# Gated attention feeding eight experts on one core: x written by engines instead of small transfers, outer products 128 wide, the plan made anew, the last plain products spread over the first groups

## The chip, the cores and the metric

The program runs on one core of a Trainium2 chip. The metric is the device time of one execution in microseconds (us). A median over several executions is compared; a profile shows one execution. The engines are TensorE (PE, with its weight loads listed as PEld), VectorE (DVE), ScalarE (ACT), GpSimd (POOL), and SyncE (SP), which here only issues DMA transfers.

## The reference

Gated linear attention over 4 batches, 8 heads, 768 tokens and 48 channels, and behind it 8 experts whose outputs are mixed with weights that come from eight rounds of row and column scaling:

```
f = sigmoid(f_logit)
for t in range(S):                       # per batch and head, state is 48 x 48
    state = f[t][:, None] * state + k[t][:, None] * v[t][None, :]
    y[t] = q[t] @ state
x = y as [3072 tokens, 384]
P = exp(x @ w_gate - max); 8 times: P /= rowsum; P /= colsum; P *= N / E
out = sum over e of P[:, e] * (relu(x @ w1[e]) @ w2[e])      # w1 384 x 1024, w2 1024 x 384
```

## The kernel before

All large products are made of float16 pairs, a high and a low part, as three matmuls (high by high, high by low, low by high), summed in float32 in PSUM.

**The stages.** The order of the instructions of every engine is fixed in the program. A first stage follows the string `PLAN`, a list of words that each emit one step of one stream. There are 24 tiles of 128 tokens (six per batch), and each tile `i` has the streams `L` (loads), `K` (keys), `d` (decays), `Q`, `V`, `A` (scores), `S` (states), `c` (carried state), `Y` (output y and x), `g` (gate logits), all in `attend`. `F` emits plain products of experts on tokens that are ready, namely those of expert 0 and of half of expert 1; they are the filler of the plan. `E` and `D` emit their evictions. `C0` to `C3` (`convert`) turn the x of a batch into sums of blocks; `B` is the scaling chain of the expert weights; `k0` and `k1` prepare the first expert weights of the second stage. After the word `X`, behind the last tile, the buffers of the attention are given back.

The second stage runs 52 periods (`period`), one per entry of `ORDER`. Each has 15 slots with six matmuls each, which are products by a scheme that forms 15 products of sums of blocks; the second half of an expert (`paired`) follows 21 slots behind. `EVENTS` says which engine step comes behind which slot, and further jobs are hung on slots by `at_all` with the lists `W1AT`, `W2AT0`, `CONVAT` and so on. The last 24 plain products are held back from the plan and emitted in the first nine slots by the counts in `HELD`.

**A token tile on its way.** `outer(c)` forms the products of keys and values in the PSUM tile `kvps`: per half of a tile 12 matmuls with a stationary operand that is R = 112 columns of `ktb`, the turned keys, wide, and 48 moving columns. The state, with the carried one, goes by DVE and ACT into `sh` and `sl`, and `outputs` collects 48 matmuls into the PSUM tile `yps`. It has one buffer, like `kvps`. Then x is written as `xh` and `xl` (float16, 128 rows: 96 rows of the first three blocks of `yps`, and three pieces of 32 rows out of its fourth block, which have to land on rows 96 to 127). In the first six tiles ACT writes the four parts of `xh` and DVE the four parts of `xl`. From tile `X3_FROM` = 6 on the 96 rows of the fourth block go into a staging tile `x3` first (one ACT, one DVE instruction), and six transfers issued by SP move its pieces of 32 rows to their places. `gates` then multiplies x by the gate weights, into spare columns of the same `kvps` buffer; the next tile's `outer` needs that buffer.

The matmuls of all these are issued through one helper (L374), the ACT steps of a tile through L648, its DVE and POOL steps through L651 and L654, and the transfers of x at L827.

Of the kernel before, what the change touches and what calls it, by code (L numbers as in the profile page):

```python
# [60 lines left out]
L0 L1 a0 a1 a2 B a3 a4 a5 a6 a7 G z K0 K0 W24 K0 K0 Z Z V0 Z V0 K0 Z K0 V0 V0 K0 V0 K0 V0 K0 K1 d0 T0 U0 V1 W3 K0 z Q0 V1 T0 T0 W3 d0 T0 Q0 U0 U0 S0  # L61
L2 Q0 W4 S0 U0 Q0 S0 c0 S0 S0 V1 A0 S0 c0 V1 V1 W9 K1 A0 V1 a0 K1 A0 K1 a0 K1 Y0 d1 Y0 a1 A0 b0 Q1 K1 Y0 d1 Y0 a2 Y0 Q1 Y0 S1 a1 Y0 Y0 Y0 Y0 F2 Q1 F2
Y0 F3 b1 F1 K1 F3 Q1 F1 Y0 Y0 K1 Y0 F1 K1 F1 a3 F3 L3 T1 U1 F4 T1 F1 K1 F6 U1 F5 a2 F3 a4 T1 A1 a3 E T1 D a5 a4 U1 a6 F8 a5 F3 b2 F1 U1 F7 a7 F5 a6 F2
b3 F7 K2 F5 a7 F1 E F3 V2 F1 D F1 G F3 V2 V2 F3 V2 A1 V2 F1 g0 K2 F2 g0 V2 F1 S1 A1 K2 c1 K2 F1 K3 A1 Y1 Y1 V3 F2 S1 F1 K2 S1 F2 E d2 Y1 c1 b0 K2 S1
V3 S1 S1 Q2 S1 Y1 Y1 K2 Q2 Y1 K2 K2 Y1 L4 U2 K2 Y1 T2 Y1 Y1 F2 Q2 Y1 F5 Y1 F1 T2 T2 Y1 Q2 F2 Y1 F2 U2 F2 b0 g1 T2 F2 U2 F2 d2 F1 A2 U2 S2 V3 F2 g1 F3
A2 V3 F1 S2 c2 V3 S2 F3 A2 F1 S2 F5 c2 F4 S2 F3 A2 Y2 Y2 E F5 V3 F3 D F5 S2 F1 Y2 F1 S2 F1 K3 F3 Y2 S2 Y2 b1 F4 K3 F3 Y2 F1 K3 F4 Y2 F3 E b1 F1 d3 F2
Y2 F1 Y2 F1 Y2 K3 F1 D F3 d3 Y2 b2 F1 S3 F2 Y2 F1 Y2 F1 b3 F1 Y2 F1 K3 F3 K4 g2 b2 F2 K3 F8 g2 F1 b3 E F7 K3 K3 F10 V4 F8 K4 F3 V4 F6 K3 E F9 V4 F3 D
F5 V4 F8 V4 F3 K3 F6 E F8 V4 F3 D F5 Q3 F13 K4 K4 F4 E F5 D K4 d4 F3 Q3 F1 d4 F3 K4 F1 Q3 L5 F1 S3 F1 K4 Q3 S3 F1 K4 F1 S3 K4 F1 S3 F1 Q4 F1 A3 K4 F2
c3 F1 S3 F2 A3 F5 E F6 Q4 F2 A3 F1 S4 F2 K4 F6 S3 S3 F2 L6 F6 Q4 F2 Y3 A3 F2 K5 Y3 S3 F2 E F1 Q4 F1 Y3 V5 F1 D F1 K5 Y3 F1 A4 V5 V5 V5 K5 Y3 V5 F2 Y3
V5 F1 A4 F1 Y3 F7 E F7 Y3 F2 Y3 F3 Y3 Y3 F3 A4 F6 Y3 F3 Q5 Y3 F4 Y3 F2 A4 F1 E F3 Q5 K5 g3 K5 Y4 d5 F1 D F1 d5 Q5 Y4 F2 g3 K6 K5 Y4 F2 K6 Q5 S4 F1 K5  # L70
S4 S4 F1 S4 F1 E F1 c4 F1 S4 K6 F1 S5 F2 S4 F2 K5 F2 S4 F1 K5 F1 V6 Y4 F4 E S4 Y4 F2 Q6 F10 K6 F2 K6 K5 F9 V6 F1 V6 F7 V6 F2 Y4 F2 E F1 d6 F2 K5 F2 L7
F4 Y4 F1 A5 D Y4 Y4 Y4 Y4 F2 V6 F6 Y4 F1 V6 F3 Y4 F3 Y4 F2 d6 F2 A5 F8 E F2 g4 Q6 F4 A5 F5 D F3 Q6 F8 g4 F1 A5 F2 Y5 K7 F4 Y5 K6 S5 K7 F1 Y5 Q6 K6 S5
F2 S5 F1 E S5 F2 K7 F1 S5 F3 S5 F2 K6 K6 F1 D F3 V7 Y5 S5 F1 K7 K7 F1 Y5 K6 F1 Q7 F1 S5 F6 d7 F1 K6 F1 L8 E F1 V7 A6 V7 V7 K7 Y5 F1 V7 F1 A6 F1 Y5 F3
Q7 Y5 F1 Y5 F1 Y5 F1 A6 Y5 F7 E F1 Y5 F4 Y5 F2 V7 F1 C0 F1 Y5 F3 A6 F3 K7 F7 g5 K7 Y6 g5 F4 Y6 Q7 K7 F3 S6 E Q7 Y6 S6 d7 K8 F2 K7 D F8 V8 F2 S6 F5 c6
F3 S6 F2 C0 V8 F2 K7 F1 S6 F1 L9 F3 V8 F2 A7 V8 Y6 K8 F5 S7 F1 Y6 F1 E F5 S6 F4 V8 F3 C0 F5 V8 F1 D F11 A7 F7 E S6 F2 C0 F1 A7 F1 D F2 K9 F1 Y6 C0 A7
F2 Y6 F1 Y6 F1 Y6 F1 K8 K8 F1 K9 F6 Y6 F1 d8 Q8 F2 C0 C0 F2 E F1 Y7 C0 K8 F1 Q8 g6 Y7 d8 C0 F1 g6 F1 K8 Q8 Y7 F1 C0 F1 S7 F1 K9 K9 S7 K8 F3 K8 F1 K8
F7 E F6 V9 F1 S7 F5 S7 F2 K9 F9 K8 F5 c7 F5 E V9 F8 S7 F6 S8 F2 K8 S7 F2 L10 F5 D F1 V9 F6 d9 F2 V9 F2 S7 Y7 F1 E F3 Y7 S7 F2 V9 F4 D F3 V9 F6 Y7 K9
d9 F5 Y7 F2 Y7 F1 Q8 F6 K9 F2 Y7 F1 C0 C0 F1 E F1 A8 Q9 C0 D F1 K9 F1 K9 F1 Y7 F1 K10 F2 A8 F1 K10 F2 K9 g7 Q9 F1 A8 F2 g7 F1 K10 Q9 F2 C0 F1 K9 K10
L11 Y8 S8 Y8 S8 A8 F1 K10 d10 F2 C0 F1 S8 V10 F1 S8 F2 E Y8 c8 F1 S8 F1 V10 F1 S9 F1 S8 F1 S8 F2 V10 F6 E Y8 S8 F2 V10 F2 Y8 K10 F2 V10 F7 V10 Y8 Q9
F5 Y8 F2 C0 C0 Y8 F7 K10 F3 A9 C0 Y8 K10 F2 Y8 K10 F4 E F4 A9 F4 Q10 F7 D F1 K10 F2 A9 F8 Q10 F1 d10 F2 K11 F6 g8 A9 C0 Y9 K10 E L12 F4 Y9 g8 Q10 C0 D  # L80
# [24 lines left out]
K22 F1 Y19 F1 d22 E F2 Y19 Y19 F1 D F2 K22 F1 Y19 F2 d22 F1 E K22 F2 Q22 F2 D Y20 K22 F1 Q22 F1 Y20 K22 F1 K22 g19 Y20 E g19 F2 A21 F1 D F1 S20 K22
Q22 F1 A21 S20 K23 F1 S20 F2 S20 V22 F1 K22 F1 c20 F1 E F1 V22 S21 F1 S20 F2 D F1 S20 F1 S20 F2 V22 F1 S20 F1 E F1 Y20 Q22 V22 F2 Y20 V22 D F2 V22 Y20
# [239 lines left out]
def fast(ctx, tc, qkf, vbd, wg, w1, w2, out, flag):  # L346
# [140 lines left out]
    def put(e, u, t, ps):  # L487
# [6 lines left out]
        if t == TT - 1:  # L494
            over.add((e, u))
# [472 lines left out]
    def convert(b, raw_left):  # L968
# [15 lines left out]
        if not planned[0]:  # L984
            yield
# [531 lines left out]
```

## Time and profile before

| | us |
|---|---|
| median of 3 runs | 1539.29 (1539.0 to 1542.9) |
| the profiled execution | 1545.27 |
| its span, first to last instruction | 1543.5 |
| TensorE busy in it | 1477.4 |

The first 381 us hold the attention (the last logits of a tile are reduced at 381.0), from there to 467 us run the rest of the plain products beside the scaling chain, and at 467 us the periods begin. The busy times by stretch show how far each engine is filled; the table of waits says what ended TensorE's idle time; the timeline shows single steps. A matmul's listed duration includes its way through the array, so that neighbours overlap: the distance between their starts is what one costs TensorE.

### The profile page before, as it was taken

What the parts mean: (1) busy time and instruction counts of PE and PEld (TensorE: products, weight loads), DVE (VectorE), ACT (ScalarE), POOL (GpSimd) and SP (SyncE); (2) the same over time, 40 slices, a digit from 0 to 9 for tenths busy, and PEclk for the clock granted to TensorE, in tenths of its full rate; (3) what the DMA queues carried; (4) which work ended last, traced back from release to release, by engine and by line L of the source; (5) the groups of instructions that cost most, each with busy time, mean ns of one, the idle gap of its engine ahead of it and who ended that gap; (6) DMA issues with size and microseconds to landing.
All of it is one profiled execution on the core that took longest, in us unless ns stands there. A gap on an engine that the chain in (4) does not pass through costs nothing.

```text
span 1543.5 us, 41018 instructions
## 1 busy us (share of the span) xinstructions
PE 1477.4 (96%) x16128; PEld 1302.3 (84%) x16128; DVE 1256.5 (81%) x2549; ACT 1157.3 (75%) x2600; POOL 1062.2 (69%) x1259
## 2 busy tenths in 40 slices
PE   8898889988999999999999999999999999999997
PEld 5776766665567899999999999999999999999997
DVE  6887777664946998888999998888888888888876
ACT  8886887763337778888888888887777778777774
POOL 3234343312725569999999999999888888888763
PEclk9999999999999999999999999999999999999999
DMA  8354435521111012222111111111000000000012
GB/s 255 89 131 117 120 96 120 130 77 32 37 42 47 12 28 58 59 59 58 58 53 58 53 49 52 51 45 37 22 13 21 22 12 22 22 22 22 1 48 81
DMA packets 87419, 89.87 MB, mean 58 GB/s; under 512 B 54992, under 2 KB 74576, under 8 KB 87216
## 3 DMA queue, kind: packets, MB, share of 16 engines
q1 hardware_dynamic: 86784, 86.57, 20.2%
q8 instruction: 128, 2.10, 0.6%
q14 instruction: 75, 0.61, 0.1%
q10 hardware_dynamic: 432, 0.59, 0.1%
HBM read 62.46 MB, written 14.16 MB: 50 GB/s over the span
## 4 chain that ended last, share of the span: by engine, by line
PE 75%; DVE 5%; ACT 3%; DMA 3%; SPq 2%; issue 1%; ACTq 0%; DVEq 0%
PE kyps L374 29%; PE kb_A L374 9%; PE kb_B L374 8%; PE kb_D L374 6%; PE kxps L374 5%; PE kb_C L374 4%; PE hps L374 4%; PE yps L374 4%; PE kb_E L374 2%; PE kb_F L374 2%; PE kvps L374 2%; DMA xl<-x 2%; SPq L827 2%; DMA xh<-x 1%; ACT vh L648 0%
## 5 line engine op out<-in xcount | busy, mean ns | idle before, releaser
L374 PEld LDWEIGHTS <-k1h 128*128 128x128 f16 x3120 | 293.7, 98 | 27.4 <-issue 6.1
L374 PE MATMUL kyps<-k2h,kgh 128*128 128x192 f16 x1248 | 307.3, 246 | 1.5 <-ACT kyps L1219 1.5
L374 PE MATMUL kyps<-k2l,kgh 128*128 128x192 f16 x1248 | 307.4, 246 | 0.0
L374 PE MATMUL kyps<-k2h,kgl 128*128 128x192 f16 x1248 | 307.4, 246 | 0.0
L374 PEld LDWEIGHTS <-kgh 128*128 128x128 f16 x2496 | 230.0, 98 | 8.8 <-issue 1.8
L1392 POOL TENSOR_TENSOR kgl<-kf,kgh 128x512 f16<-128x512 f32 x153 | 205.7, 1345 | 2.5 <-ACT kgh L1389 2.5
L1222 DVE SCALAR_TENSOR_TENSOR yy<-kyps,pes,part 128x192 f32<-128x192 f32 x282 | 116.9, 415 | 101.2 <-PE kyps L374 91.1
L1392 POOL TENSOR_TENSOR kgl<-kr,kgh 128x512 f16<-128x512 f32 x153 | 182.2, 1191 | 11.5 <-PE kyps L374 9.9
L1261 POOL TENSOR_TENSOR acc<-acc,yy 128x384 f32<-128x384 f32 x141 | 141.1, 1001 | 67.7 <-DVE yy L1222 67.7
L374 PEld LDWEIGHTS <-k1l 128*128 128x128 f16 x1560 | 152.8, 98 | 17.8
L374 PEld LDWEIGHTS <-kh 128*128 128x128 f16 x1248 | 117.3, 98 | 8.9 <-issue 2.1
L374 PEld LDWEIGHTS <-kgl 128*128 128x128 f16 x1248 | 122.2, 98 | 0.1
L651 POOL TENSOR_TENSOR kb<-q,kb 48x512 f16<-48x512 f32 x42 | 51.8, 1234 | 86.4 <-ACT kb L648 85.1
L1343 ACT ACTIVATE cp<-kb_A 128x512 f32<-128x512 f32 x156 | 93.5, 599 | 20.0 <-DVE kb_A L1345 18.3
L1369 POOL TENSOR_TENSOR kr<-kr 128x256 f32<-128x256 f32 x104 | 78.0, 750 | 44.1 <-ACT kr L1358 41.7
L1219 ACT ACTIVATE kyps<-kyps 128x192 f32<-128x192 f32 x156 | 50.2, 322 | 73.0 <-PE kyps L374 70.9
L1389 ACT ACTIVATE kgh<-kf 128x512 f16<-128x512 f32 x156 | 98.7, 633 | 0.4 <-DVE kf L1366 0.4
L1389 ACT ACTIVATE kgh<-kr 128x512 f16<-128x512 f32 x156 | 98.1, 629 | 0.0
L374 PEld LDWEIGHTS <-w1h 128*128 128x128 f16 x1008 | 75.6, 101 | 25.0 <-issue 5.5
L374 PE MATMUL yps<-w2l,hh 128*128 128x384 f16 x288 | 95.9, 333 | 0.0
L374 PE MATMUL yps<-w2h,hl 128*128 128x384 f16 x288 | 95.9, 333 | 0.1
L374 PE MATMUL yps<-w2h,hh 128*128 128x384 f16 x288 | 95.6, 332 | 0.0
(287 smaller groups left out, 5531.2 us busy)
## 6 DMA issues: line engine op xcount, KB each, us to landing
q<-in_qkf_dram SPq DMA_DIRECT2D x23, 672.0 KB, 5.9
k1r<-in_w_dram SPq DMA_DIRECT2D x26, 384.0 KB, 3.0
k2r<-in_w_dram SPq DMA_DIRECT2D x26, 384.0 KB, 3.0
ys<-yr SPq DMA_DIRECT2D x48, 192.0 KB, 2.0
yb<-ys SPq DMA_DIRECT2D x48, 192.0 KB, 2.4
vr<-in_vbd_dram SPq DMA_DIRECT2D x24, 192.0 KB, 3.7
out_dram<-acc SPq DMA_DIRECT2D x21, 192.0 KB, 1.9
w1r<-in_w_dram SPq DMA_DIRECT2D x6, 384.0 KB, 8.5
```

The lines of the kernel that those rows point to most:

```text
L374: ins = (nc.tensor.transpose if transpose else nc.tensor.matmul)(**kw)
L651: pin(eng.tensor_tensor(out=out, in0=in0, in1=in1, op=op))
L827: nc.sync.dma_start(out=x[96:128, n, tok], in_=x3[32 * n:32 * n + 32, q, :])
L1219: pin(nc.scalar.activation(out=out, in_=in_, func=AF.Copy, **kw))
L1222: pin(nc.vector.scalar_tensor_tensor(out=y, in0=ps, scalar=p, in1=z, op0=ALU.mult, op1=ALU.add))
L1261: pin(nc.gpsimd.tensor_tensor(out=y, in0=y, in1=z.rearrange("p s d -> p (s d)"), op=ALU.add))
L1343: pin(nc.scalar.activation(out=fresh(ev[2]), in_=bk, func=AF.Copy))
L1369: pin((nc.gpsimd if ev[2] == 'P' else nc.vector).tensor_tensor(out=r[:, 0], in0=r[:, 1], in1=r[:, 0], op=ALU.subtract))
L1389: pin(nc.scalar.activation(out=hs['g', t][0][i], in_=hs['f' if i else 'r', t], func=AF.Copy))
L1392: pin((nc.vector if tag == str(PERIODS - 1) else nc.gpsimd).tensor_tensor(out=hs['g', t][1][i], in0=hs['f' if i else 'r', t], in1=hs['g', ...
```

## The change

In `outputs`, all 24 tiles write x the way the first six do: four ACT and four DVE instructions, no staging tile, no transfers. A step of the plan is one of these, so that the `Y` stream of tiles 6 to 23 has 14 steps in place of 10. `outer` takes a stationary operand 128 columns wide from tile 3 on (the first three tiles, turned by TensorE, stay at 112); the 16 further columns belong to the next block and their results are not read.

The plan is new over its whole length, with the same streams. Plain products ahead of the last tile's gate logits: 1855 before, 1875 after; in the whole plan 2352 before, 2340 after. Two new streams `k2` and `k3` prepare the first w2 weights in the plan (nine steps each); before they hung on the slots of the first period (`W2AT0`, `W2AT1`). Those weights get buffers of their own (`k2p`). The last conversion steps of batch 3 move from the second period to the first (`CONVAT`). A plain expert's tokens count as free when its first product is done, no longer when its second is. The 36 last plain products, in place of 24, are held and spread over the first 19 slots; the buffers that open behind them are split in two pools (`lq`). A check that tokens are ready is now made per block.

```diff
-HELD = (0, 1, 6, 2, 6, 3, 2, 4, 0)
-X3_FROM = 6
+HELD = (0, 0, 0, 0, 1, 1, 2, 2, 2, 3, 3, 3, 3, 3, 3, 3, 3, 2, 2)
-W2AT0 = (1, 1, 1, 2, 3, 4, 4, 4, 6)
-W2AT1 = (2, 8, 9, 11, 11, 12, 12, 12, 15)
-CONVAT = (0, 1, 6, 10, 12, 14, 15, 22, 24, 24, 26, 33, 35)
+CONVAT = (0, 1, 2, 3, 4, 5, 6, 7, 8, 9, 10, 11, 12, 13, 14)
...
         def outer(c):
-            kv = o["kv"][:, c]
+            kv, wide_ = o["kv"][:, c], R if by_pe else 128
...
-                    mm(out=kv[0:R, p, :], lhsT=ktb[i % 2][:, w:w + R], rhs=x[:, c * NP + p, :], start=(m == 0), stop=(m == 2))
+                    mm(out=kv[0:wide_, p, :], lhsT=ktb[i % 2][:, w:w + wide_], rhs=x[:, c * NP + p, :], start=(m == 0), stop=(m == 2))
...
-            parts = PCS
-            if i >= X3_FROM:
-                parts = PCS[:1]
-                x3 = new("x3", [96, 2, TS], F16, bufs=1)
-                act(x3[:, 0, :], yps[0:96, 3], scale=YS * XS)
-                yield
-            for n, (si, so) in enumerate(parts):
+            for n, (si, so) in enumerate(PCS):
                 act(xh[so + (tok,)], yps[si], scale=YS * XS)
...
-            if i >= X3_FROM:
-                three(x3[:, 1, :], yps[0:96, 3], YS * XS, x3[:, 0, :], ALU.mult, ALU.subtract)
-                for q, x in enumerate((xh, xl)):
-                    for n in range(3):
-                        nc.sync.dma_start(out=x[96:128, n, tok], in_=x3[32 * n:32 * n + 32, q, :])
-                ready.add((u, s % TT, 0))
-                yield
-            for n, (si, so) in enumerate(parts):
+            for n, (si, so) in enumerate(PCS):
                 three(xl[so + (tok,)], yps[si], YS * XS, xh[so + (tok,)], ALU.mult, ALU.subtract)
...
+    streams.update((f"k{2 + n}", prepare_w2(ORDER[0][0], 2 * ORDER[0][1] + n)) for n in range(2))
...
-        if n == 0:
-            at_all(0, W2AT0, prepare_w2(e, 2 * m))
-            at_all(0, W2AT1, prepare_w2(e, 2 * m + 1))
...
-    at_all(1, CONVAT, converts[3])
+    at_all(0, CONVAT, converts[3])
```

## Rows read from the trace of the kernel before

**Rows 1.** The page of the profile: the span, the busy time of each engine over it, and the clock granted to TensorE in 40 equal slices (tenths of full speed).
```profile
span 1543.5 us, 41018 instructions
...
PE 1477.4 (96%) x16128; PEld 1302.3 (84%) x16128; DVE 1256.5 (81%) x2549; ACT 1157.3 (75%) x2600; POOL 1062.2 (69%) x1259
...
PEclk9999999999999999999999999999999999999999
```

**Rows 2.** The busy time of each engine in six stretches of the span that follow one another. Columns: stretch and its length in us, busy us of PE, of the weight loads (PEld), of DVE, ACT and POOL, each with its number of instructions; then the granted clock of TensorE as a share, the busy share of the DMA engines and GB/s.
```profile
0.00:61.00 61.00, 48.57 (x597) 35.47 (x598) 44.26 (x81) 51.19 (x105) 19.11 (x36) 0.92 0.59 180
61.00:121.00 60.00, 56.31 (x912) 47.22 (x910) 50.76 (x79) 51.80 (x111) 23.19 (x22) 1.00 0.55 137
121.00:381.00 260.00, 227.57 (x2844) 166.72 (x2842) 170.42 (x304) 180.30 (x387) 82.21 (x98) 0.93 0.40 98
381.00:467.00 86.00, 83.52 (x520) 50.67 (x519) 58.64 (x121) 30.31 (x64) 43.14 (x61) 1.00 0.11 39
467.00:540.00 73.00, 67.36 (x637) 58.71 (x635) 60.84 (x118) 55.09 (x121) 42.02 (x55) 0.98 0.10 31
540.00:1543.50 1003.50, 994.02 (x10629) 943.47 (x10627) 871.52 (x1848) 788.62 (x1816) 852.58 (x990) 1.00 0.13 39
```

**Rows 3.** What TensorE's matmuls waited for in the stretch from 121 to 381 us. Columns: us in total, number of waits, the longest. `kvps` with `xl` or `xh` is a matmul of the gate logits; `yps` is the output of a token tile.
```profile
PE kvps L374 <- DMA xl<-x: 20.4, 43, 1.9
PE kvps L374 <- DMA xh<-x: 7.8, 9, 1.9
PE yps L374 <- DVE xl L654: 2.1, 4, 1.4
```

**Rows 4.** The timeline of SyncE's DMA issues around 170 us: start, duration in us, what, how many.
```profile
168.01 1.79 SPq L827 DMA_DIRECT2D xh<-x  x3
169.91 1.80 SPq L827 DMA_DIRECT2D xl<-x  x3
171.80 2.75 SPq L491 DMA_DIRECT2D ys<-yr  x2
```

**Rows 5.** The timeline of TensorE around 338 us: start, duration, matmul, and in brackets the idle time ahead of it with its releaser.
```profile
337.26 0.18 PE L374 MATMUL kvps<-wgs,xl 128*128 128x16 f16 x1 [0.46 <-DMA xl<-x]
...
338.59 0.18 PE L374 MATMUL kvps<-wgs,xl 128*128 128x16 f16 x1 [0.47 <-DMA xl<-x]
```

**Rows 6.** The busy times in slices of 3.4 us (columns as in Rows 2, the granted clock third from the end). Between 121 and 381 us 18 slices, in eight stretches, show a clock under 1.00; the first two, two in the middle and the last of these are given.
```profile
125.80:129.20 3.40, 2.38 (x28) 1.82 (x28) 1.91 (x3) 1.16 (x2) 0.55 (x2) 0.75 0.16 58
129.20:132.60 3.40, 3.40 (x30) 2.79 (x30) 1.07 (x3) 0.30 (x2) 2.01 (x2) 0.50 0.00 0
...
336.60:340.00 3.40, 1.96 (x24) 1.34 (x25) 1.72 (x4) 0.91 (x3) 0.59 (x1) 0.87 0.21 68
340.00:343.40 3.40, 3.40 (x32) 2.83 (x31) 0.47 (x2) 1.47 (x4) 0.00 (x0) 0.63 0.16 58
...
370.60:374.00 3.40, 3.40 (x19) 1.89 (x18) 1.82 (x4) 1.53 (x3) 0.00 (x0) 0.61 0.00 0
```

**Rows 7.** The costliest groups of weight loads from 0 to 640 us, shapes kept apart. `kt` is the turned keys of the outer products (112 columns), `kb` the keys of the scores (128 columns). Columns: busy us, mean ns of one, idle before.
```profile
L374 PEld LDWEIGHTS <-kt 128*112 128x112 f16 x576 | 41.5, 150 | 4.6 <-issue 2.1
...
L374 PEld LDWEIGHTS <-kb 112*128 112x128 f16 x624 | 24.0, 101 | 4.3 <-issue 2.5
```

**Rows 8.** The timeline of TensorE around 161 us. The first two rows bound one half of a tile's outer products (12 matmuls, then other work), the last two the scores of a tile (24 matmuls, then other work).
```profile
160.41 0.26 PE L374 MATMUL kvps<-vhc,kt 128*112 128x48 f16 x2
...
161.03 0.27 PE L374 MATMUL hps<-xl,w1h 128*128 128x128 f16 x2
...
162.12 0.22 PE L374 MATMUL aps<-qh,kb 112*128 112x64 f16 x2
...
162.82 0.84 PE L374 MATMUL hps<-xh,w1l 128*128 128x128 f16 x12
```

**Rows 9.** The timeline of ACT at token tile 3, whose x is written by engines already.
```profile
78.91 0.49 ACT L648 ACTIVATE xh<-yps 96x384 f16<-96x384 f32 x1
...
79.80 0.85 ACT L648 ACTIVATE xh<-yps 32x128 f16<-32x128 f32 x3
```

**Rows 10.** The timeline of DVE at the same tile: the low parts of x, four instructions in one row.
```profile
80.68 1.49 DVE L654 SCALAR_TENSOR_TENSOR xl<-yps,xh 96x384 f16<-96x384 f32 x4 [1.82 <-ACT xh L648]
```

**Rows 11.** The timeline of ACT at a later tile, whose last 96 rows go by transfers: the staging tile `x3` (printed as `x`), then `xh`.
```profile
167.72 0.26 ACT L648 ACTIVATE x<-yps 96x128 f16<-96x128 f32 x1
167.88 0.48 ACT L648 ACTIVATE xh<-yps 96x384 f16<-96x384 f32 x1
```

**Rows 12.** The timeline of DVE at the same later tile.
```profile
168.40 0.29 DVE L654 SCALAR_TENSOR_TENSOR x<-yps,x 96x128 f16<-96x128 f32 x1 [0.58 <-ACT xh L648]
...
169.20 0.55 DVE L654 SCALAR_TENSOR_TENSOR xl<-yps,xh 96x384 f16<-96x384 f32 x1
```

**Rows 13.** What TensorE's matmuls waited for from 61 to 121 us, where x is written by engines for nearly all of it (columns as in Rows 3).
```profile
PE yps L374 <- ACT sh L648: 1.4, 1, 1.4
PE kvps L374 <- DVE xl L654: 1.0, 2, 0.7
```

**Rows 14.** What TensorE's matmuls waited for from 467 to 540 us (columns as in Rows 3).
```profile
PE kb_A L374 <- ACT cp L1343: 2.4, 4, 1.4
PE kb_D L374 <- DVE kf L1366: 1.1, 2, 0.6
PE kb_D L374 <- DVE kb_F L1348: 0.9, 2, 0.7
```

More of the change, by code (lines that the diff above doesn't have):

```diff
@@ L65 @@
[L65 to L68, printed above, removed]
@@ L477, in evicted, with need @@
             yield
-    def need(u, parts, low):
-        if not all((u, t, low) in ready for t in parts):
+    def need(u, parts, low, k):
+        if not all((u, t, low, k) in ready for t in parts):
             raise RuntimeError("an expert is ahead of its tokens")
@@ L493, in put @@
         evict("E", op)
-        if t == TT - 1:
-            over.add((e, u))
     def moe_up(e, u, h, to=FT):
@@ L505, in moe_up @@
             for a, x in ((wh, xh), (wl, xh), (wh, xl)):
-                need(u, range(TT), int(x is xl))
                 for k in range(KT):
+                    need(u, range(TT), int(x is xl), k)
                     mm(out=ps, lhsT=a[:, k, fs], rhs=x[:, k, :], start=(n == 0), stop=(n == 8))
@@ L517, in moe_up @@
             hl.append(tl)
+            if f == FEATS[e] - 1:
+                over.add((e, u))
             yield 1
@@ L538, in tile_up @@
         w1s = ws[e][0]
-        need(u, (t,), 0)
         xh, xl = xof(u)
@@ L560, in tile_up @@
             h.append([v.rearrange("p (f t) -> p f t", t=128) for v in (th, tl)])
+            if t == TT - 1 and g == FEATS[e] // 4 - 1:
+                over.add((e, u))
             yield 1 / 3
@@ L811, in outputs @@
                 yield
-            parts = PCS
-            if i >= X3_FROM:
-                parts = PCS[:1]
-                x3 = new("x3", [96, 2, TS], F16, bufs=1)
-                act(x3[:, 0, :], yps[0:96, 3], scale=YS * XS)
-                yield
-            for n, (si, so) in enumerate(parts):
-                act(xh[so + (tok,)], yps[si], scale=YS * XS)
-                if n == len(PCS) - 1:
-                    ready.add((u, s % TT, 0))
-                yield
-            if i >= X3_FROM:
-                three(x3[:, 1, :], yps[0:96, 3], YS * XS, x3[:, 0, :], ALU.mult, ALU.subtract)
-                for q, x in enumerate((xh, xl)):
-                    for n in range(3):
-                        nc.sync.dma_start(out=x[96:128, n, tok], in_=x3[32 * n:32 * n + 32, q, :])
-                ready.add((u, s % TT, 0))
-                yield
-            for n, (si, so) in enumerate(parts):
+            for n, (si, so) in enumerate(PCS):
+                act(xh[so + (tok,)], yps[si], scale=YS * XS)
+                ready.add((u, s % TT, 0, n - 1))
+                yield
+            for n, (si, so) in enumerate(PCS):
                 three(xl[so + (tok,)], yps[si], YS * XS, xh[so + (tok,)], ALU.mult, ALU.subtract)
-                if n == len(parts) - 1:
-                    ready.add((u, s % TT, 1))
+                ready.add((u, s % TT, 1, n - 1))
                 yield
@@ L982, in block @@
             return sums[n // 9][:, n % 9, :].rearrange("p (u t) -> p u t", u=2)
-        if not planned[0]:
-            yield
         for i, (r, p, op, q) in enumerate(XSUMS):
             pin((nc.vector if b in SUMS_BY_DVE else nc.gpsimd).tensor_tensor(out=block(r), in0=block(p), in1=block(q), op=ALU.add if op == '+' else ALU.subtract))
-            if planned[0]:
-                yield
+            yield
             if i in (1, 5, 9):
@@ L992, in convert @@
                 pin(nc.vector.tensor_reduce(out=xmx[:, b, k:k + 1], in_=x32[:, k].rearrange("p u t -> p (u t)"), axis=AX.X, op=ALU.max, apply_absolute_value=True))
-                if planned[0]:
-                    yield
-            if i % 2 and not planned[0]:
                 yield
-        if not planned[0]:
-            yield
         xb = [xqs[b // 2].tile([128, 6, 256], F16, name=f"xb{n}{b}") for n in "hl"]
@@ L1002, in convert @@
                 pin(nc.scalar.activation(out=dst[:, 4 + n, :].rearrange("p (u t) -> p u t", u=2), in_=src[:, q // 3, :, 128 * (q % 3):128 * (q % 3) + 128], func=AF.Copy, scale=sign))
-                if planned[0]:
-                    yield
-            if not planned[0]:
                 yield
-        if not planned[0]:
-            yield
         while raw_left() > 0:
@@ L1018, in convert @@
                 pin(nc.scalar.activation(out=dst[0][:, lo:hi, :], in_=sums[n][:, lo:hi, :], func=AF.Copy))
-                if planned[0] and i:
+                if i:
                     yield
@@ L1083, in prepare_w2 @@
         yield
-        wh, wl = (lp.tile([128, 7, DH], F16, name=f"k2{n}_{e}_{j}", tag=f"k2{n}", bufs=4) for n in "hl")
+        place = len(turns) % 4
+        turns.append(place)
+        wh, wl = ((k2p if place < 2 else lp).tile([128, 7, DH], F16, name=f"k2{n}_{e}_{j}", tag=f"k2{n}{place}", bufs=1) for n in "hl")
         (b11, b12), (b21, b22) = ((raw[:, f, 0:DH], raw[:, f, DH:DM]) for f in range(2))
@@ L1158, in fast @@
             kw = ctx.enter_context(tc.tile_pool(name="kw", bufs=4, reuse_waits="tile"))
+            k2p = ctx.enter_context(tc.tile_pool(name="k2p", bufs=1, reuse_waits="tile"))
         elif word[0] == "F":
@@ L1178, in fast @@
     late.append(lp)
-    lq = []
+    lq = [ctx.enter_context(tc.tile_pool(name="lq", bufs=1, reuse_waits="tile"))]
     acc = {}
@@ L1192, in paired @@
         x0, y0, x1 = q[:, 0:DH], p[:, 0:DH], p[:, DH:DM]
-        p2 = lq[0].tile([128, DH], F32, name=f"part_{n}_{t}", tag="part", bufs=2)
+        p2 = lq[1].tile([128, DH], F32, name=f"part_{n}_{t}", tag="part", bufs=2)
         by_pool = t in BY_POOL and n < len(ORDER) - 1 and not new
@@ L1387, in event @@
                 else:
-                    hs['g', t] = [[lq[0].tile([128, 2, 2, 128], F16, name=f"kg{q}{i}_{tag}_{t}", tag=f"kg{q}{t}{i}", bufs=1) for i in range(2)] for q in "hl"]
+                    hs['g', t] = [[lq[t].tile([128, 2, 2, 128], F16, name=f"kg{q}{i}_{tag}_{t}", tag=f"kg{q}{t}{i}", bufs=1) for i in range(2)] for q in "hl"]
             pin(nc.scalar.activation(out=hs['g', t][0][i], in_=hs['f' if i else 'r', t], func=AF.Copy))
@@ L1425, in period @@
             ps = ctxt[0][bk]
-            if not lq:
-                for _ in range(HELD[s]):
+            if len(lq) < 2:
+                for _ in range(HELD[n * PRODUCTS + s]):
                     next(kept[0])
-                if s == len(HELD) - 1:
+                if n * PRODUCTS + s == len(HELD) - 1:
                     if next(kept[0], kept) is not kept:
@@ L1432, in period @@
                     wctx2.close()
-                    lq.append(ctx.enter_context(tc.tile_pool(name="lq", bufs=1, reuse_waits="tile")))
+                    lq.append(ctx.enter_context(tc.tile_pool(name="lq2", bufs=1, reuse_waits="tile")))
             for c in range(2):
```

124 lines of the change are left out of this document (63 added, 61 removed).

## The prediction

> **What bounds the kernel now.** Start with the page: TensorE is busy for 1477.4 of 1543.5 us, no other engine for more than 81%, so the question is where TensorE stands still or runs slowly [rows 1]. The busy times by stretch answer it [rows 2]. From 540 us on TensorE is idle for 9.5 of 1003.5 us at full clock, and the diff leaves the steps of that stretch alone: nothing is to be won or lost there. From 381 to 467 us it is idle for 2.5 of 86. The attention is the loose part: 12.4 us idle in the first 61, 3.7 in the next 60, 32.4 in the 260 from 121 to 381, where the clock is also granted at only 0.93. The start of the periods (467 to 540) has 5.6 us of idle.
>
> The table of waits then says what the 32.4 us are: 20.4 for transfers into `xl` and 7.8 for transfers into `xh`, both ahead of gate matmuls, so 28.2 of them belong to the transfers of x [rows 3]. The timeline shows why: SP needs 1.8 us to issue three transfers, 3.7 us for the six of a tile, and `xl` goes last [rows 4]; TensorE has reached the gate matmuls by its fixed order and stands before each of them for nearly half a microsecond [rows 5]. And the clock: all of the missing 7% of this stretch lies in eight short ones, at or on the way to the lower level, 1.2 GHz of 2.4. In the two whose beginning is shown, TensorE is busy for 2.38 and 1.96 of 3.4 us in the first slice, in the second of them idle at gate matmuls, and then fully busy at a low clock [rows 5, 6]. From 61 to 121 us, with 6% idle in smaller pieces, the clock is 1.00 [rows 2].
>
> **The change part by part.**
>
> *Transfers of x removed.* The 28.2 us of waits go [rows 3]. What is late next? In the 60 us from 61 to 121, where nearly every x is written by engines, TensorE was idle for 3.7 us, 6.2% [rows 2], by waits on ACT and DVE, 1.0 us of them gate matmuls on `xl` [rows 13]. I take that share as the idle time of the new stretch: 6.2% of about 220 us are 13 us. So idle falls from 32.4 to 13: a gain of 19 us. The bounds: 28 if nothing takes the place of the transfers, and a gain of nothing if each tile finds another wait. SP also loses 108 issues of some 0.6 us; the stores of `yr` behind them go earlier [rows 4], and I count nothing for that.
>
> *Clock.* 260 us at 0.93 are 18 us of full-speed work lost [rows 2]. If the long stops at the gates cause the drops, the clock should stay up as it did from 61 to 121. A new plan will leave some stops; I take 11 of 18. Bounds 0 and 18.
>
> *Outer products 128 wide.* Twelve of them take 160.41 to 161.03, so 52 ns each; 24 score matmuls with a stationary operand of 128 columns, and even more moving columns, take 162.12 to 162.82, 29 ns each [rows 8]. The listed weight loads agree: 150 ns for 112 columns, 101 for 128 [rows 7]. 21 tiles of 24 matmuls are 504; at 23 ns less each 11.6 us. They lie on TensorE's own path and ahead of the state, hence no cover; some sit in time that was slack, and I take 10. The bounds are 0 and 12.
> The Trainium skill, in TensorE: Matmul & The Clock Gate, section LDWEIGHTS (loading the stationary operand), has the time of a weight load grow with the columns, P / 1.2 ns, which would be 107 ns for 128 and 93 for 112 and speaks against this edit; by it the edit would cost an estimated 7 us (504 times 13 to 14 ns) where the rows give 10 back. Its section on weight-path modes says that a fast load is on when the number of weights is 128 and the type is not float32; the rows side with that.
>
> *Pieces added on ACT and DVE.* At tile 3 the three 32-row pieces take ACT 0.85 us [rows 9]; they replace the staging step of 0.26 [rows 11]: 0.59 more, over 18 tiles 10.6 us. DVE needs 1.49 us for its four parts [rows 10] and before 0.29 + 0.55 [rows 12]: 0.65 more, 11.7 us. Neither is on TensorE's path as long as the engine keeps up: ACT is busy for 180.3 of 260 us, and 190.9 of a shortened 220 would be 87%, DVE 182 of 220, 83%. From 61 to 121 they ran at 86% and 85% with TensorE at 94% [rows 2]. So the end of 220 is just what ACT has been seen to carry, and this is the tightest point of the forecast. What if the cover is gone? Then ACT sets the length; that is the first rival.
>
> *The start of the periods.* Of the 5.6 us idle from 467 to 540 the largest are waits on copies and subtractions that ACT and DVE do late, 2.4, 1.1 and 0.9 us [rows 14], while they also prepare the first w2 weights and convert batch 3. Two w2 preparations leave for the plan, and 12 more plain products (0.16 us each) are spread where TensorE stood. A gain of 3 us; bounds 6 and minus 2, because the conversion now falls into the first period whole. In the plan the w2 steps run beside plain products after 381 us, where ACT has 56 us and DVE 27 of 86 free [rows 2]; I cost them at nothing. If that room were not there, they would bring the waits that they have a part in now, at most 5.6 us, back at an earlier place.
>
> *Plan and bookkeeping.* The same plain products run, 20 more ahead of the last gate logits (3 us, moved, not added). The first 61 us, with 12.4 us idle and a clock of 0.92, are replanned too; the diff has no new cause there, so 0, between minus 5 and plus 5.
>
> *Sum.* 19 + 11 + 10 + 3 = 43 us. The profiled execution took 1545.3 us, so it would take 1502; the median of the runs is 6.0 us lower than it, which gives 1496.
>
> **The rivals.**
>
> *ACT binds.* The gaps in ACT's order do not close as well as from 61 to 121, and it fills only 80%: 190.9 / 0.80 = 239 us for this stretch, a gain of 21, with the 3 of the periods 24: 1515. For it: ACT is the fullest engine beside TensorE in the attention, and its work grows. Against it: it waits for TensorE behind the same gates now, and those waits shrink.
>
> *Everything comes in.* No new waits and no drop of the clock: 28 + 18 + 12 + 5 = 63, 1476. Against it stands the 6% idle of the stretch that already works so.
>
> *The weight load grows with its columns.* 128 columns are 14% more than 112. If an outer product costs that much more, 52 ns become 59, and 504 of them lose 3.7 us in place of a gain of 10: the sum is 29 and the time 1510. Against it speak the scores, which have 128 columns and take 29 ns [rows 7, 8].
> The load rule of the Trainium skill's page TensorE: Matmul & The Clock Gate, cited above, works in this direction; its mode rule and the trace agree against it.
>
> *The gain is filled up again.* The new order puts an equal stop elsewhere, and the time stays within 0.3% of 1539.3 (1534.7 to 1543.9, about what a measurement of this kernel can tell from no change).
>
> *Slower: the single `yps` buffer.* The last reader of `yps` is now the fourth piece on DVE, 0.65 us later than before in DVE's time; the next tile's 48 matmuls, and all plain products queued behind them on TensorE, stand until then. That wait exists: 2.1 us in four waits, the longest 1.4 [rows 3]. It would have to grow to 43 / 18 = 2.4 us in each of the 18 tiles, clock drops included, to eat the gain; at 3 us per tile the loss is 11, and the time 1550. For it: both engines have fixed orders and the pieces may sit behind other work. Against it: the plan can place products of plain experts ahead of `yps`.
>
> **How the numbers follow.** The forecast, 1480 to 1510, 0.53; ACT binds, 1510 to 1533, 0.25; everything comes in, 1468 to 1480, 0.09; wider loads, about 1510, 0.02; filled up, 0.05; slower, 0.06. Faster by over 0.3% is the sum of the first four, 0.89. The range of 8 in 10 takes the forecast, most of the ACT case, and the upper half of the best case: 1474 to 1526. Its width is that of three open terms: idle 0 to 28, clock 0 to 18, the start 10 either way with the first 61 us.
>
> **What would show it.** Right, in the profile after: no transfers at the line of `outputs`; no waits of `kvps` on `xh` or `xl` from a DMA; weight loads of `kt` near 100 ns and twelve outer products in 0.35 us; logits of the last tile near 341 us in place of 381, with a granted clock of 0.97 or more up to there; ACT near 87% in the attention; the periods from about 427 us on, 1003 us of tail unchanged. Wrong: waits of `yps` on `xl` from DVE in most tiles, waits on `sh` from ACT that add up to more than 13 us, clock drops at new places, or a tail that changes its length.

## The result, and the profile after

The changed kernel takes 1489.8 us (median of 4, 1489.2 to 1490.7); the kernel before took 1541.1 beside it. The ratio is 0.966, with a 95% interval of 0.963 to 0.969: about 51 us less. The profiled execution took 1490.65 us. The page of the changed kernel, as [rows 1]:

```profile
span 1488.8 us, 40831 instructions
...
PE 1444.7 (97%) x16125; PEld 1276.8 (86%) x16125; DVE 1274.0 (86%) x2585; ACT 1167.7 (78%) x2636; POOL 1060.1 (71%) x1259
...
PEclk9999999999999999999999999999999999999999
```

TensorE is less busy by 32.7 us and the span is 54.7 us shorter, so 22 us of the gain is idle time of TensorE that is gone; the rest is work that runs faster. (The profiled execution of the kernel before is 4 us above its median, hence 54.7 here and 51 by the medians.) The stretches are cut near the events of [rows 2] (the logits of tile 2, of the last tile, the first period); only the row behind the cut at 108 us has another partner, which follows below:

```profile
0.00:56.00 56.00, 46.53 (x581) 34.17 (x582) 43.81 (x77) 49.91 (x103) 16.69 (x34) 0.94 0.62 193
56.00:108.00 52.00, 46.92 (x760) 37.90 (x760) 39.33 (x70) 42.83 (x94) 15.06 (x17) 0.97 0.53 132
108.00:340.60 232.60, 213.68 (x3029) 154.83 (x3027) 200.98 (x353) 201.29 (x444) 89.65 (x105) 0.99 0.47 113
340.60:418.40 77.80, 77.80 (x488) 47.59 (x487) 63.75 (x128) 32.90 (x69) 48.52 (x65) 1.00 0.18 57
418.40:491.40 73.00, 71.77 (x712) 64.59 (x711) 61.63 (x125) 55.42 (x124) 43.36 (x56) 1.00 0.05 16
491.40:1488.80 997.40, 988.00 (x10566) 937.75 (x10563) 864.54 (x1835) 785.40 (x1807) 846.79 (x984) 1.00 0.14 40
```

At 108 us stand the logits of tile 5 (107.7). In the kernel before these come at 110.0 us, not at 121. So the partner of the long stretch from 108 to 340.6 us is this row of before:

```profile
110.10:381.20 271.10, 238.20 (x3016) 175.63 (x3013) 179.28 (x317) 188.95 (x405) 90.50 (x107) 0.94 0.41 102
```

The plan also shifts plain products between the stretches (1250 stand between the gates of tile 5 and the last ones in the old plan, 1291 in the new). The rows from the start to the last logits are free of that, but for the 20 more products that now stand ahead of them; first before, then after:

```profile
0.00:381.20 381.20, 332.65 (x4349) 249.53 (x4350) 265.62 (x464) 283.29 (x601) 124.71 (x156) 0.94 0.45 118
```

```profile
0.00:340.60 340.60, 307.13 (x4366) 226.90 (x4367) 284.12 (x499) 294.02 (x638) 121.40 (x155) 0.98 0.50 129
```

Up to the last logits TensorE's idle time falls from 48.6 to 33.5 us and its busy time from 332.7 to 307.1. The last logits are reduced at 340.4 us, before at 381.0: 40.6 us. The first matmul of the periods comes at 418.5 us, before at 467.3: from the last logits to it 78.1 us in place of 86.3, and from it to the end 1070.3 in place of 1076.2. So 40.6 + 8.2 + 5.9 make up the 54.7. The last row, from 73 us behind the first period, hardly differs in its idle time: 9.4 us, before 9.5. It is 6 us shorter than in [rows 2] because some 60 fewer matmuls are left for it: 712 in place of 637 run in the 73 us ahead of it. DVE and ACT are now busy for 86.4% and 86.5% of the long stretch, before 66% and 70%.

The waits of TensorE's matmuls from 108 to 340.6 us, against [rows 3] (columns as there):

```profile
PE yps L374 <- ACT sh L642: 6.1, 8, 1.6
PE kvps L374 <- DVE lg L825: 3.1, 3, 1.9
PE kvps L374 <- DVE xl L648: 2.6, 6, 0.7
PE yps L374 <- DVE sl L648: 2.1, 4, 1.0
...
PE yps L374 <- DVE xl L648: 0.4, 1, 0.4
```

No gate matmul waits for a transfer any more. What is late next is the state (`sh`, `sl`), the logits that hold the `kvps` buffer, and only then x itself. The wait of `yps` on the last reader of its buffer, the mechanism of the slower rival, is 0.4 us. The weight loads of the outer products, against [rows 7], and one half of a tile's twelve, against [rows 8] (first row its start, second the work behind it):

```profile
L374 PEld LDWEIGHTS <-kt 128*128 128x128 f16 x504 | 17.7, 97 | 8.7 <-issue 7.3
```

```profile
166.05 0.21 PE L374 MATMUL kvps<-vhc,kt 128*128 128x48 f16 x2
...
166.35 0.27 PE L374 MATMUL hps<-xh,w1h 128*128 128x128 f16 x2
```

97 ns for a load in place of 150, and twelve matmuls in 0.30 us in place of 0.62: 25 ns each.

### The profile page after: what moved, and what is told of

Read it like the earlier page. It is cut to its first block, busy times and chain, and to the rows that moved or that the text cites. A ratio compares the mean times of both kernels' runs of the same rounds, so it can differ in the third digit from the quotient of the medians.

```text
span 1488.8 us, 40831 instructions
## 1 busy us (share of the span) xinstructions
PE 1444.7 (97%) x16125; PEld 1276.8 (86%) x16125; DVE 1274.0 (86%) x2585; ACT 1167.7 (78%) x2636; POOL 1060.1 (71%) x1259
## 4 chain that ended last, share of the span: by engine, by line
PE 78%; ACT 9%; DVE 7%; DMA 4%; issue 2%; SPq 0%; ACTq 0%; DVEq 0%
PE kyps L374 30%; PE kb_A L374 9%; PE kb_B L374 9%; PE kb_D L374 7%; PE kxps L374 5%; PE kb_C L374 5%; PE yps L374 4%; PE hps L374 4%; DMA q<-in_qkf_dram 3%; PE kb_E L374 2%; PE kb_F L374 2%; ACT xh L642 1%; DVE xl L648 1%; DVE sl L648 1%; ACT kb L642 1%
## 5 line engine op out<-in xcount | busy, mean ns | idle before, releaser
L1356 ACT ACTIVATE kgh<-kf 128x512 f16<-128x512 f32 x156 | 98.6, 632 | 0.4 <-DVE kf L1333 0.4
```

The lines of the kernel that those rows point to most:

```text
L1356: pin(nc.scalar.activation(out=hs['g', t][0][i], in_=hs['f' if i else 'r', t], func=AF.Copy))
```

## The experiments

Eleven kernels were run, in three sets, each set beside the kernel before, which took 1543.1, 1546.4 and 1540.5 us in them (1541.1 beside the changed kernel). The changed kernel was not run again in the sets. A distance to it of 2 or 3 us by the times alone is therefore not safe; the ratio to before and the profile have to agree. "Old plan" is the plan of before, "new plan" that of the changed kernel.

**Transfers back, new plan.** Tiles 6 to 23 go by the staging tile and six transfers again; the plan, its steps and all else as changed.

```diff
             for n, (si, so) in enumerate(PCS):
-                act(xh[so + (tok,)], yps[si], scale=YS * XS)
+                if not far or not n:
+                    act(xh[so + (tok,)], yps[si], scale=YS * XS)
+                elif n == 1:
+                    act(x3[:, 0, :], yps[0:96, 3], scale=YS * XS)
+                    for m in range(3):
+                        nc.sync.dma_start(out=xh[96:128, m, tok], in_=x3[32 * m:32 * m + 32, 0, :])
...
```

(`far` is `i >= 6`; the same for `xl`.)

> The changed kernel with the transfers of x put back for tiles 6 to 23 (one ACT and one DVE staging instruction, six transfers per tile), all else as changed, the new plan too. Theory that the removed transfers carry the gain: gate matmuls wait for the transfers again, 20 to 30 us of idle plus clock drops, less what ACT and DVE save: 1515 to 1530 us. Rival, that the new plan carries it and hides the transfers: at most 1500 us.

Measured: 1559.4 us, ratio to before 1.011 (1.006 to 1.015). That is 70 us behind the changed kernel, more than either theory said, and slower than the kernel before. The long stretch, and the waits in it:

```profile
108.00:405.80 297.80, 239.97 (x3018) 173.12 (x3015) 185.88 (x317) 191.70 (x408) 86.99 (x105) 0.89 0.38 92
```

```profile
PE kvps L374 <- DMA xh<-x: 32.7, 24, 6.8
PE kvps L374 <- DMA xl<-x: 19.9, 33, 4.7
```

The gate matmuls stand for 52.6 us, nearly twice as long as under the old plan (28.2, [rows 3]), and the clock falls to 0.89: 11% of 298 us are 33 us of full-speed work lost. The gate matmuls stand closer behind the transfers: under the old plan 12 to 16 plain products stood between the step that issues those of `xl` and the gates in 16 of the 18 tiles, in this run 7 to 10 in 14 of them. One tile in the timelines of SP and of TensorE:

```profile
225.43 1.79 SPq L815 DMA_DIRECT2D xh<-x  x3
227.32 0.52 SPq L653 DMA_DIRECT2D q<-in_qkf_dram  x1
227.98 0.34 SPq L657 DMA_DIRECT2D vr<-in_vbd_dram  x1
228.43 2.06 SPq L824 DMA_DIRECT2D xl<-x  x3
```

```profile
227.19 0.18 PE L374 MATMUL kvps<-wgs,xh 128*128 128x16 f16 x1 [1.41 <-DMA xh<-x]
...
233.28 0.42 PE L374 MATMUL kvps<-wgs,xl 128*128 128x16 f16 x3 [4.69 <-DMA xl<-x]
```

Between the two groups of transfers SP issues the load of the next tile's decays, keys and queries, 672 KB. The transfers of `xl`, issued last, are waited for 4.69 us. At 177 us, where the load was issued ahead of all six, the wait is the longest, 6.8 us. So the gain of the transfers' removal belongs to the plan that it stands in. The 70 us are the price of the transfers as this run places them: behind the 96 rows and in two groups, where the kernel before filled the staging tile first and issued all six together. That no other placing would do better under the new plan is not shown.

**Outer products 112 wide again, new plan.**

```diff
-            kv, wide_ = o["kv"][:, c], R if by_pe else 128
+            kv, wide_ = o["kv"][:, c], R
```

> The changed kernel with outer products 112 wide again. Theory: 504 matmuls at 52 in place of 27 ns put 12 us on TensorE's path: 1499 to 1503 us. Rival, that they lie in slack: at most 1493 us.

Measured: 1495.3 us (1494.6 to 1496.5), ratio 0.969 (0.965 to 0.972), 5.5 us behind the changed kernel; its last logits come at 346.3 us, 5.9 later. Between the two theories. The long stretch shows where the other half is (behind it the row from the start to the last logits):

```profile
108.00:346.40 238.40, 224.64 (x3048) 168.21 (x3045) 202.02 (x355) 202.53 (x446) 90.97 (x106) 0.99 0.46 111
0.00:346.40 346.40, 319.03 (x4366) 240.76 (x4366) 282.24 (x499) 294.69 (x638) 122.28 (x155) 0.98 0.50 127
```

TensorE is busy 11 us longer (224.6 against 213.7) and idle for 13.8 us, in the changed kernel for 18.9. So the wide products take 11 us off TensorE's work, and half of that comes back as idle time, as other engines end the waits.

**x by engines alone, old plan.** Of the ten steps of `Y` the four last write the 96 rows of `xh`, its three pieces, the 96 rows of `xl`, its three pieces (the lines as they run from tile 6 on).

```diff
-                act(x3[:, 0, :], yps[0:96, 3], scale=YS * XS)
-                yield
-            for n, (si, so) in enumerate(parts):
-                act(xh[so + (tok,)], yps[si], scale=YS * XS)
+            for part in (PCS[:1], PCS[1:]):
+                for si, so in part:
+                    act(xh[so + (tok,)], yps[si], scale=YS * XS)
+                yield
...
```

> The kernel before, under its old plan, with x written by engines in all tiles: the step of the staging instruction becomes the 96 rows of xh, the next the three pieces, and so for xl; nothing else. Theory that the transfers carry the gain: 25 to 33 us less than before, 1506 to 1515 us. Rival, that it takes a new plan: the old order has other waits in their place, at least 1530 us.

Measured: 1519.4 us, ratio 0.984 (0.980 to 0.988), about 24 us less than before: just short of the theory's range, and far from the rival. The stretch from 121 us to the last logits, as in [rows 2], and its waits:

```profile
121.00:358.80 237.80, 210.85 (x2845) 156.21 (x2844) 186.97 (x341) 193.31 (x424) 81.89 (x98) 0.97 0.43 103
```

```profile
PE yps L374 <- DVE xl L654: 17.1, 12, 3.0
PE yps L374 <- ACT kb L648: 3.7, 1, 3.7
```

The 28.2 us of waits on transfers are gone and the clock is up from 0.93 to 0.97. But 27 us of idle are left of 32.4, and 17.1 of them are a wait that stood at 2.1 in [rows 3]: the next tile's `yps` matmuls for the last reader of the one buffer.

**Both parts, old plan.** The run above with `outer` 128 wide as in the change.

> The kernel before, under its old plan, with x written by engines and outer products 128 wide. Theory that these two carry the gain: 35 to 43 us less than before, 1497 to 1505 us, and the new plan with the moved steps the rest. Rival, that the plan does: at least 1525 us.

Measured: 1516.4 us, ratio 0.982 (0.978 to 0.986): some 27 us less than before, of 51. Both theories miss: the parts bring half, and the plan with the moved steps the other half. The waits again, and one of them in the timelines of TensorE and DVE:

```profile
PE yps L374 <- DVE xl L654: 19.3, 12, 3.1
PE yps L374 <- ACT kb L648: 4.4, 1, 4.4
```

```profile
193.84 0.41 PE L374 MATMUL yps<-ah,vh 128*128 128x64 f16 x8 [1.86 <-DVE xl L654]
```

```profile
192.29 1.49 DVE L654 SCALAR_TENSOR_TENSOR xl<-yps,xh 96x384 f16<-96x384 f32 x4 [2.90 <-ACT xh L648]
```

DVE stands for 2.90 us until ACT has written `xh`, needs 1.49 us for the four parts of `xl`, and TensorE, which has the next tile's products with `vh` next in its order, stands for 1.86 us until the last of them has been read out. This wait has grown by 2.2 us beside the run before, so a part of what the wide products give ends in it. The two times say that they bring 3 us here, not 12; the traces say 7. This profiled execution reached the logits of tile 0, ahead of anything that the wide products touch, at 38.7 us, the run before at 35.4, and its clock up to 61 us was 0.86, there 0.92. From the logits of tile 0 to those of the last tile it takes 316.0 us, the run before 323.2.

**Outer products 128 wide alone, old plan.** The two lines of the change in `outer`, transfers as before.

> The kernel before, under its old plan and with its transfers, with outer products 128 wide alone. Theory: 10 to 12 us off TensorE's path, 1527 to 1531 us. Rival: TensorE gains them and stands longer ahead of the gate matmuls, whose transfers come no sooner: at least 1536 us.

Measured: 1529.3 us (1528.6 to 1538.0), ratio 0.991 (0.988 to 0.994): some 13 us less than before by the ratio. Here they count in full: the last logits come at 367.4 us, 13.6 sooner, and the waits for the transfers are the same in size.

**Pieces pulled ahead, old plan.** As both parts under the old plan, with the three pieces of `xh` in the step of its 96 rows, and so for `xl`; the steps behind are empty.

> The old plan with both parts (x by engines, outer products 128 wide) as in the run before, but the three pieces of xh pulled up to the step of its 96 rows, and those of xl likewise, so that the last reader of yps comes one plan step sooner. With both parts the old plan gave 1516 us and 19.3 us of waits of yps on xl. If the single yps buffer is what takes the gain back there, those waits fall by 5 to 12 us and so does the time: 1504 to 1511 us. Rival, that the engines as such are too slow: pulled pieces delay what stood ahead of them, at least 1514 us.

Measured: 1512.0 us, ratio 0.982 (0.979 to 0.984), which can't be told from the run without it. The waits moved:

```profile
PE yps L374 <- DVE xl L654: 13.2, 11, 1.9
PE kvps L374 <- DVE lg L843: 4.6, 9, 1.0
```

6 us less at `yps`, 4 us more at the logits that hold `kvps` (0.7 in the run with both parts). From the logits of tile 0 to those of the last tile it is 313.9 us against 316.0. The time lies between the theory and the rival. So the wait at `yps` alone is not the whole limit of the old plan; with it shortened by a third, others come last. What its full removal would bring under the old plan is not shown.

**Held products in nine slots, new plan.**

```diff
-HELD = (0, 0, 0, 0, 1, 1, 2, 2, 2, 3, 3, 3, 3, 3, 3, 3, 3, 2, 2)
+HELD = (0, 2, 9, 3, 9, 4, 3, 6, 0)
```

> The changed kernel with its 36 held products in the first nine slots, in place of 19. Theory that the spread fills stops of TensorE in the first periods: 1 to 3 us more, 1491 to 1493 us, and idle of 3 us or more from the first period on for 73 us, in place of 1.2. Rival, that the stops are gone for other reasons: within 0.7 us of the changed kernel.

Measured: 1493.1 us (1491.4 to 1494.5), 3.3 behind the changed kernel by the times; the ratio, 0.966 (0.963 to 0.968), is that of the changed kernel. The profile decides for the theory. The first 73 us of the periods, and from the first period to the end:

```profile
419.90:492.90 73.00, 70.00 (x687) 62.17 (x685) 58.97 (x120) 54.88 (x122) 41.40 (x54) 1.00 0.04 15
419.90:1492.70 1072.80, 1060.37 (x11275) 1002.21 (x11272) 925.68 (x1959) 841.63 (x1930) 890.36 (x1040) 1.00 0.13 38
```

TensorE is idle for 3.0 us in the 73, in the changed kernel for 1.2, and from the first period to the end it takes 1072.8 us in place of 1070.3: 2.5 us.

**The w2 preparations on their old slots, new plan.** `k2` and `k3` leave the plan, `W2AT0` and `W2AT1` return.

> The changed kernel with the two w2 preparations of the first period taken out of the plan and hung on their old slots. Theory that they cause the waits on copies and subtractions in the first periods: 2 to 5 us more, 1492 to 1495 us. Rival, that ACT and DVE have room for them there: within 0.7 us.

Measured: 1492.6 us (1491.5 to 1493.5), 2.8 behind the changed kernel by the times; here too the ratio, 0.966 (0.963 to 0.968), can't be told from that of the changed kernel. By the profile it is 2.4 us from the first period to the end, the lower end of the theory:

```profile
418.10:1490.80 1072.70, 1060.11 (x11274) 1002.25 (x11272) 930.38 (x1966) 844.33 (x1935) 893.79 (x1044) 1.00 0.14 39
```

**All three moves undone, new plan.** The two above, and the last conversion in the second period again.

> The changed kernel with all three moves at the start of the periods undone: 36 products in the first nine slots, the two w2 preparations on their old slots, the last conversion in the second period. Alone the first cost 3.3 and the second 2.8 us. If they fill different stops, 6 to 8 us more than the changed kernel, 1496 to 1498 us; if the same ones, 3 to 4 us, 1493 to 1494 us.

Measured: 1498.4 us (1497.7 to 1500.6), ratio 0.973 (0.971 to 0.975), 8.6 behind the changed kernel. The row from 418.4 us for 73, one from the first period to the end, and the two largest waits in the former:

```profile
418.40:491.40 73.00, 66.33 (x637) 57.83 (x636) 60.46 (x118) 54.66 (x119) 42.37 (x53) 1.00 0.10 31
419.30:1496.40 1077.10, 1060.78 (x11274) 1002.16 (x11272) 931.53 (x1966) 844.98 (x1936) 897.07 (x1044) 1.00 0.13 39
```

```profile
PE kb_A L376 <- ACT cp L1314: 2.4, 2, 1.4
PE kb_D L376 <- DVE kb_F L1319: 1.9, 2, 1.7
```

6.7 us idle, and 5.6 in [rows 2] with [rows 14]; the changed kernel has 1.2. From the first period to the end it is 6.8 us more than in the changed kernel, where the first two moves alone cost 2.5 and 2.4. So these two fill different stops; the rest, 1.9 us, would be the conversion's, which was not run alone.

**Loads in three transfers, new plan.** In the changed kernel ACT waits for the loads of decays, keys and queries, here from 108 to 340.6 us (us in total, times, longest):

```profile
ACT q L642 <- DMA q<-in_qkf_dram: 8.4, 8, 1.8
```

```diff
-            if i:
-                nc.sync.dma_start(out=q3, in_=qkf[i].rearrange("r n p t -> r n (p t)"))
-            else:
-                for n in (0, 2, 1):
-                    nc.sync.dma_start(out=q3[:, n, :], in_=qkf[i, :, n].rearrange("r p t -> r (p t)"))
+            for n in (0, 2, 1):
+                nc.sync.dma_start(out=q3[:, n, :], in_=qkf[i, :, n].rearrange("r p t -> r (p t)"))
```

> The changed kernel with the load of each tile's decays, keys and queries cut into three transfers, decays first, as tile 0 has it. In the trace of the changed kernel the chain of waits holds these loads for 15% of its time from 108 to 340 us. If they set the pace there, decays that land 2 us sooner give 2 to 8 us: 1482 to 1488 us. If the chain only passes through them because TensorE and ACT are full, no change within 1 us, or a loss by the two more issues on SP.

Measured: 1482.0 us (1480.3 to 1484.1), ratio to before 0.959 (0.957 to 0.962), 8 us less than the changed kernel by the times, 11 by the ratios. The same wait of ACT in this run, from 102 us (tile 5) to 328.8 (the last logits):

```profile
ACT q L642 <- DMA q<-in_qkf_dram: 0.9, 2, 0.7
```

The last logits come at 328.6 us, 11.8 sooner. Half of that is gained before the logits of tile 5 already (101.9 us in place of 107.7): there the changed kernel has one wait of 2.2 us for the logits that hold `kvps`, with a drop of the clock behind it, and this run has 0.45 us and a clock of 1.00. From the first period to the end this execution takes 2 us longer, for no reason that a run shows.

**Loads in two transfers, new plan.** Decays first, keys and queries together.

> The changed kernel with the load cut in two, decays first, keys and queries together. If early decays are what gave 8 us in the run with three transfers, the same: 1480 to 1484 us. If the early keys count too, 1484 to 1488 us.

Measured: 1480.8 us (1480.2 to 1482.3), ratio 0.961 (0.959 to 0.964). ACT's wait:

```profile
ACT q L642 <- DMA q<-in_qkf_dram: 1.4, 2, 1.1
```

The early decays are enough; early keys add nothing that can be told. These two are faster than both kernels; between them nothing can be told.

## Why the prediction was right

The forecast was 43 us less, the ratio says 51 to 52. The direction, the place and the end of the attention (341 us forecast, 340.4 measured) came out. That the end of the attention fits so well is in part luck, as terms missed in both directions. The steps one by one:

*Transfers and clock (19 + 11 us).* From the logits of tile 5 to the last ones the idle time fell from 32.9 to 18.9 us, where I took 13 as left: 14 in place of 19. The clock missed the other way: summed over slices as in [rows 6], 17.1 us of full-speed work lost became 1.7, 15 in place of 11. Together 29 against 30. That long stops at the gates go with a low clock was right from both sides: without the transfers it is 0.99 here and 0.97 under the old plan, and with the transfers back under the new plan the waits rise to 52.6 us and the clock falls to 0.89. One of my signs of being wrong did show: the clock fell at a new place, to 0.62 from 95.2 to 98.6 us, behind the wait of 2.2 us for logits; in [rows 2] it was 1.00 there.

*Outer products (10 us).* The mechanism and the pace were right (52 ns to 25). What they are worth depends on what stands behind: 13 us under the old plan with the transfers, 7 us by the traces behind the wait at `yps`, 5.5 us in the changed kernel. A term that I sized once had three sizes. The rule of the Trainium skill in TensorE: Matmul & The Clock Gate, section LDWEIGHTS (loading the stationary operand), that a load's time grows with its columns, is not borne out across the step from 112 to 128: 97 ns at 128 columns, 150 at 112; the rival that went with it is out.

*Up to the last logits (40 us).* The rows give 15 us of idle time and 25.5 of busy time. The busy part is near 15 of the clock and 12 of the outer products (the run with 112 columns is busy for 319.0 us up to its last logits, the changed kernel for 307.1), less 3 for the 20 more plain products. I had counted those as moved, at no cost, but they do lie in this stretch.

*Pieces on ACT and DVE.* 86.5% and 86.4% busy, where I had 87% and 83%, and 86% and 85% from 61 to 121 us as what has been seen [rows 2]. The rival in which ACT binds at 80% did not come. But ACT's order is part of what limits the stretch: 6.1 us of TensorE's waits are for `sh` from ACT, and with ACT's waits for loads shortened the kernel gets 8 us faster.

*The slower rival, the single `yps` buffer.* Its mechanism is real: under the old plan the wait grows from 2.1 to 17.1 and 19.3 us. It doesn't reach the 2.4 us per tile that would eat the gain (17.1 / 18 is 1.0). Under the new plan it is 0.4 us. I weighed it as a rival of the whole change; it is rather one thing that the new plan was needed against. Shortening it from 19.3 to 13.2 us under the old plan gained nothing that can be told from noise, as other waits grew by 4 us and more; so the plan probably did more than this one thing, but no run removes the wait whole.

*The start of the periods (3 us, bounds 6 and minus 2).* Under-sized, and beyond my bound: undoing all three moves costs 8.6 us by the times and 6.8 by the profile from the first period on, 5.7 of it idle time. The bound was the idle time of 5.6 us in [rows 2]; with 36 products in the nine slots it is 6.7. The w2 steps, costed at nothing, cost nothing that shows at their new place: TensorE is busy for all of the 77.8 us from 340.6 to 418.4 us.

*From 381 to 467 us (nothing).* It gave 8.2 us. 20 plain products now run ahead of the last logits and 12 in the periods: 32 of 0.163 us are 5.2 us, moved, as I wrote; the other 3 us are the 2.5 us of idle that I had counted as staying, with little else.

*The plan.* I gave it no term of its own, and here the working was weak: with both parts and the old plan the kernel takes 1516 us, with the new plan but the period's moves undone 1498, with them 1490. So the two parts alone bring some 27 us, the new order of the attention with its bookkeeping 14 (by the ratios) to 18 (by the times), and the moves 7 (by the profile) to 10 (by the ratios). My sum came out near because I sized the parts as they would be under a plan made for them, by the row of a stretch where x was already written by engines. What exactly in the new order brings the 14 to 18 us stays open beyond the wait at `yps` and the clock; no run took single steps of it apart.

## What to carry to other kernels

Removing a wait under a fixed order moved most of it here to the next buffer with one copy: 28 us of waits went and 15 came there. Size the removal and the new order as one change, and look for the row where the kernel already works in the new way, because that row holds the waits that stay. Judge a stop on TensorE with the clock that follows it: here the clock was worth as much as the idle time. When the runs stand in different sets, as the small moves of the periods did, compare stretches of the profiles and not only times. And when a load is what the chain shows next, cut it so that the part that is needed first lands first: one line gave 8 us more.

## What the runs showed of the hardware

A piece of 32 rows and 128 columns out of PSUM costs ACT and DVE as much as 96 rows of the same width. The changed kernel's pieces (instructions, us in total, ns of one):

```profile
L642 ACT ACTIVATE xh<-yps 32x128 f16<-32x128 f32 x72 | 19.1, 266 | 1.5
L648 DVE SCALAR_TENSOR_TENSOR xl<-yps,xh 32x128 f16<-32x128 f32 x72 | 20.6, 287 | 1.8
```

The kernel before, its staging tile:

```profile
L648 ACT ACTIVATE x<-yps 96x128 f16<-96x128 f32 x18 | 4.8, 265 | 3.5 <-issue 2.0 <-PE yps L374 1.3
L654 DVE SCALAR_TENSOR_TENSOR x<-yps,x 96x128 f16<-96x128 f32 x18 | 5.1, 282 | 11.2 <-ACT xh L648 11.2
```

At this width the rows made no difference to the price.

Transfers of 8 KB behind a load of 672 KB were late. With the load issued ahead of all six or among them, a gate matmul waited for up to 6.8 us, where the old plan's longest such wait was 1.9 [rows 3].
